# LSH attention with a spatial-gating MLP: hash rows by way of DRAM, two softmax factors on another engine, new figures in the plan

## Chip, cores, metric

One core of a Trainium2 chip runs the whole kernel. The metric is the device time in microseconds of that core, the median of several executions of the unchanged program. Engines are named as in the profile: PE (matrix products), DVE (VectorE), ACT (ScalarE), POOL (GpSimd) and SP, whose queue issues every DMA of this kernel.

## What is computed

The reference, cut to what matters (float32 attention; batch 4, 8 heads, 768 positions, head width 64; then an MLP of model width 512 and inner width 1024):

```python
q_bits = (np.einsum('bhsd,dk->bhsk', q, proj) > 0)          # 6 hash bits; k likewise
mask = q_bucket[:, :, :, None] == k_bucket[:, :, None, :]
scores = np.where(mask, scale * np.matmul(q, k.transpose(0, 1, 3, 2)), -1000000000.0)
attn = np.exp(scores - np.max(scores, axis=-1, keepdims=True))
attn = attn / (np.sum(attn, axis=-1, keepdims=True) + 1e-09)
x = np.matmul(attn, v)                                       # heads side by side
h = np.maximum(x @ w_in, 0.0); u, v = h[..., :512], h[..., 512:]
v_n = (v - mu) / np.sqrt(var + 1e-06)
out = (u * (np.einsum('ts,bsd->btd', w_spatial, v_n) + b_spatial)) @ w_out
```

## The kernel before, in words

Heads are worked on in pairs (`pair(p)`, 16 of them, four to a batch), one head on partitions 0 to 63 and one on 64 to 127. Each operand is held as a float16 high part and a low part, and a product is three products of parts that add up in PSUM. A pair first loads its q and k (`qk`, line 282), takes the hash projection on PE (`hash_`, tile `hp`), makes signs of it on DVE (line 290, tile `sg0`), scales them on ACT (line 292, tile `sg1`), and lays them out as twelve rows a head in a buffer `hr`; `rows` (line 295) does that in eight DMAs, four pieces for each of two heads. In the scores the row parts of q times those of k enter as a fourth product, which lowers every score whose buckets differ.

A pair then has six **steps** (`scores`, line 330), one for each 128 queries; 96 in all. A step is 16 score matmuls on PE (tiles `sp`); for each of two heads `cut` on DVE, which copies the scores to SBUF (`ex`) and takes their maximum (`mx`); `nb`, the maximum times a factor (line 362, on POOL, 128x2 numbers); `exp` on ACT with sums in `sm` (line 367); `ri`, the sum made ready for the reciprocal (line 369, POOL, 128x2) and the reciprocal itself (line 370, DVE); the high part of the weights on ACT (line 373, `pp`) and the low part on DVE (line 375); and `turn`, a DMA transpose per head (line 381, `pt<-pp`). After three steps `weighted` (line 384) multiplies the transposed weights with v on PE (tile `pv`) and writes `xt`. When a batch's four pairs are done, `mlp` (line 411) has 28 units of PE work for it (`vps`, `ups`, `sps`, `ops`), which the order spreads between the next batch's steps; those of the last batch stand alone at the end. The MLP's weights are loaded and split during the first batches (`weights`, line 224, tiles `raw`).

Every operation is recorded with an engine, a duration, a due key and, for a DMA, a landing time. `plan` (line 122) then plays the queues through with these figures and the sizes of the buffer rings (`RING`, line 84), always taking the ready operation with the lowest key, and what comes out is the fixed program order of all five queues. On the chip every queue runs in that order, whatever the real durations are: an instruction that waits holds up all that stand behind it on its queue. In the plan `rows` counts as one operation of 0.6 us on SP, a transpose as 1.4 us on SP with 2.0 us to land, `nb` and `ri` as 0.25 and 0.2 us on POOL. `pp` has a ring of four, so two steps' weights can wait for their transposes; `ex` has six (three steps).

Of the kernel before, what the change touches and what calls it, by code (L numbers as in the profile page):

```python
# [14 lines left out]
P = 128  # L15
D = 64
# [16 lines left out]
def lsh_attention_spatial_gating(  # L33
# [35 lines left out]

    NHR = 3  # L70
    NR = 2 * NB
    hr = [const.tile([P, 2, S], F16, name=f"hr{i}") for i in range(NHR)]
    for i, t in enumerate(hr):
# [9 lines left out]

    RING = {"sc": 2, "pv": 2, "m": 2, "hr": NHR, "qk": 1, "v32": 1, "hl": 2, "vp": 2, "sg0": 1, "sg1": 2,
            "ex": 6, "pp": 4, "pt": 4, "xt": 6, "st2": 4, "st6": 4, "v32m": 4, "vy": 2, "vn": 1, "u": 1,
            "g": 1, "sy": 2, "sm3": 2, "bs": 2, "mv": 2}
# [35 lines left out]
    def plan():  # L122


        SEM, MODE, DMA_LAT = 0.1, 0.1, 1.6
        LATE = {"PE": 0.17, "DVE": 0.09, "ACT": 0.1, "POOL": 0.05, "SP": 0.0}
# [36 lines left out]
        while done < len(ops):  # L163
            nxt = None
            for e in free:
                while free[e] <= now:
# [57 lines left out]
    def weights():  # L224
        vi, vo, vs = (x.rearrange("(c p) f -> p c f", p=P) for x in (w_in, w_out, w_sp))
        n = 0
        for src, dst, cs, lo, hi, m, f, W, key, dk in (
                (vi, wi, NPAIR, F2, DF, 256, SX, Wv, 5.0, 1.9), (vi, wi, NPAIR, 0, F2, 256, SX, Wu, 20.5, 1.0),
                (vs, ws, NT, 0, S, HS, SW, Ws, 28.0, 0.5), (vo, wo, NF, 0, DM, 256, SX, Wo, 33.5, 0.5)):
            for c in range(cs):  # L230
                for h in range(lo, hi, m):
                    job(n, src[:, c, h:h + m], [w[:, c, h:h + m] for w in dst], m, f, W, key)
                    n += 1
                    key += dk
        op("SP", 0.5, 27.0, lambda: nc.sync.dma_start(out=bt, in_=b_sp.partition_broadcast(P)), w=[Bt], land=1.0)

    def job(n, src, dst, m, f, W, key):
# [4 lines left out]

        op("SP", 0.5, key - 1.5, fetch, w=[raw], land=1.6 if m == 256 else 1.1)
        if src.dtype == F32:
# [33 lines left out]
    def pair(p):  # L278
        b, r = divmod(p, NPAIR)
        k0 = NT * (p - 1) + 0.4 if p else -40.0  # L280
        qk, v32, hl, vp, hrb, hp, s0, s1 = (Buf(t) for t in ("qk", "v32", "hl", "vp", "hr", "m", "sg0", "sg1"))
        op("SP", 0.9, k0 - 1.9, lambda: nc.sync.dma_start(out=tile_of(qk, wk, [P, 2, S], F32, f"qk{p}"), in_=kq[b, r]), w=[qk], land=2.4)

        def hash_():
            t = tile_of(hp, ps_m, [P, 512], F32, f"hp{p}")
            matmuls([(t[32 * j:32 * j + 32, :HS], pj, qk.t[:, 1 - j // 2, (j % 2) * HS:(j % 2 + 1) * HS],
                      True, True, (0, 32 * j)) for j in range(4)])
# [6 lines left out]

        def rows():
            hrb.t = hr[p % NHR]
            for e in range(2):
                for j in range(4):
                    nc.sync.dma_start(
                        out=hrb.t[D * e:D * e + NR, 1 - j // 2, (j % 2) * HS:(j % 2 + 1) * HS],  # L300
                        in_=s1.t[32 * j + 16 * e:32 * j + 16 * e + NR, :])

        op("SP", 0.6, k0 + 0.3, rows, r=[s1], w=[hrb], land=0.8)

# [10 lines left out]
        k1 = NT * p  # L315
        op("SP", 0.5, k1 - 3.0, lambda: nc.sync.dma_start(out=tile_of(v32, wk, [P, 2 * NT, D], F32, f"v32_{p}"), in_=v[b, r]), w=[v32], land=1.3)
        op("ACT", 0.74, k1 + 0.5, lambda: nc.scalar.activation(
# [12 lines left out]
    def scores(p, i, hl, hrb, pts):  # L330
# [24 lines left out]
        for e in range(2):  # L355
# [5 lines left out]
            op("DVE", 0.88, g, cut, r=[ps[e]], w=[ex[e], mx])  # L361
        op("POOL", 0.25, g, lambda: nc.gpsimd.tensor_scalar(tile_of(nb, wk, [P, 2], F32, f"nb{p}_{i}"), mx.t, -ISQ, None, op0=ALU.mult), r=[mx], w=[nb])  # L362
        for e in range(2):
# [4 lines left out]
            op("ACT", 0.92, g, exp, r=[nb], w=[ex[e], sm])  # L368
        op("POOL", 0.2, g, lambda: nc.gpsimd.tensor_scalar(tile_of(ri, wk, [P, 2], F32, f"ri{p}_{i}"), sm.t, 1e-9, 1.0 / SP, op0=ALU.add, op1=ALU.mult), r=[sm], w=[ri])  # L369
        op("DVE", 0.1, g, lambda: nc.vector.reciprocal(ri.t, ri.t), w=[ri])  # L370
        j = i % 3
        for e in range(2):
# [5 lines left out]
            def turn(e=e):  # L378
                if j == 0:
                    tile_of(pts[e], wk, [P, 2 * NT, 3, P], F16, f"pt{p}_{i}_{e}")  # L380
                nc.sync.dma_start_transpose(out=pts[e].t[:, :, j, :], in_=pp[e].t.rearrange("p g c k -> p (g c k)"))
            op("SP", 1.4, g, turn, r=[pp[e]], w=[(pts[e], j)], land=2.0)

# [27 lines left out]
    def mlp(b):  # L411
# [111 lines left out]
        def o_unit(i, key):  # L523
# [3 lines left out]
            def product():  # L527
# [87 lines left out]
```

## Time and profile before

| | us |
|---|---|
| median of 3 runs (727.54 to 729.74) | 729.18 |
| the profiled execution, whole | 725.48 |
| its span, first to last instruction | 723.7 |
| PE / DVE / ACT / POOL busy in the span | 602.5 / 528.4 / 507.4 / 200.5 |

The whole time of the profiled execution is 1.8 us more than its span, and 3.7 us below the median. Busy times are sums over stretches with different limits; the stages are read apart below. The granted clock of PE is given as a share of its full 2.4 GHz.

### The profile page before, as it was taken

To read this page: it belongs to the slowest core of one execution; us is meant where nothing else is said; L and a number is where in the kernel's file an instruction comes from. 1 tells how busy PE (TensorE), PEld (TensorE's weight loads), DVE (VectorE), ACT (ScalarE), POOL (GpSimd) and SP (SyncE) were. 2 spreads that over 40 slices of the span, in tenths; PEclk is the share of its full clock that TensorE was granted. 3 is DMA by queue.
4 is the path that set the end of the run, shared out by engine and by line. 5 is a ranking of instruction groups with operands and counts; after the bars stand their busy time and mean duration, and the time that the engine had idled before them with its cause. 6 is when DMAs were issued, how large, how long until landed. Compare 5 with 4: busy or idle time off the path is not lost. (4 is left out here: it accounts for less than half of the span.)

```text
span 723.7 us, 12276 instructions
## 1 busy us (share of the span) xinstructions
PE 602.5 (83%) x4352; PEld 302.6 (42%) x4352; DVE 528.4 (73%) x985; ACT 507.4 (70%) x905; POOL 200.5 (28%) x322
## 2 busy tenths in 40 slices
PE   2658566658888875999899989969998999989997
PEld 0224223333444432455344545534454555445553
DVE  3869788978799889857679876985788968864100
ACT  3768577878899768856777877785768778763221
POOL 2022122233144443106014420420033502302513
PEclk9998666666999985999999999989999999999999
DMA  4677988979798779886786869779856997790011
GB/s 137 178 160 155 223 178 159 224 142 236 124 237 150 176 166 217 186 177 138 135 202 126 171 126 217 162 152 181 159 112 139 178 178 131 146 202 3 1 45 43
DMA packets 317726, 111.73 MB, mean 154 GB/s; under 512 B 304224, under 2 KB 307296, under 8 KB 317664
## 3 DMA queue, kind: packets, MB, share of 16 engines
q1 hardware_dynamic: 317664, 110.94, 74.3%
q8 instruction: 34, 0.56, 0.3%
q14 instruction: 28, 0.23, 0.1%
HBM read 27.94 MB, written 6.29 MB: 47 GB/s over the span
## 5 line engine op out<-in xcount | busy, mean ns | idle before, releaser
L214 PE MATMUL sp<-hl 64*128 64x384 f16 x1152 | 169.3, 374 | 82.6 <-DVE ex L359 79.7
L375 DVE SCALAR_TENSOR_TENSOR pp<-ex,ri,pp 128x768 f16<-128x768 f32 x192 | 199.2, 1063 | 46.9 <-ACT pp L373 46.0
L373 ACT ACTIVATE pp<-ex,ri 128x768 f16<-128x768 f32 x192 | 172.3, 927 | 56.5 <-DMA pt<-pp 21.9
L367 ACT ACTIVATE ex<-ex,nb 128x768 f32<-128x768 f32 x192 | 177.5, 925 | 42.9 <-POOL nb L362 42.8
L359 DVE TENSOR_SCALAR_CACHE_REDUCE ex<-sp 128x768 f32<-128x768 f32 x192 | 179.2, 947 | 23.6 <-PE sp L214 23.3
L214 PEld LDWEIGHTS <-hl 64*128 64x128 f16 x1152 | 66.7, 103 | 171.0 <-issue 117.8
L214 PE MATMUL pv<-pt,vp 128*64 128x384 f16 x1152 | 112.7, 350 | 10.5 <-DMA pt<-pp 10.4
L214 PE MATMUL sps<-ws,vn 128*128 128x384 f16 x576 | 98.3, 328 | 0.0
L214 PE MATMUL sp<-hr 64*128 64x384 f16 x384 | 92.3, 376 | 4.1 <-DMA hr<-sg 4.1
L214 PEld LDWEIGHTS <-vp 128*64 128x64 f16 x1152 | 70.7, 118 | 54.6 <-issue 17.3
L369 POOL TENSOR_SCALAR ri<-sm 128x2 f32<-128x2 f32 x96 | 29.3, 305 | 199.6 <-ACT ex L367 192.8
L362 POOL TENSOR_SCALAR nb<-mx 128x2 f32<-128x2 f32 x96 | 37.0, 385 | 151.6 <-DVE ex L359 129.0
L214 PEld LDWEIGHTS <-vn 128*128 128x128 f16 x576 | 54.8, 98 | 41.9 <-issue 7.6
L214 PE MATMUL ops<-wo,g 128*128 128x512 f16 x288 | 66.9, 383 | 1.8 <-POOL g L520 1.0
L214 PE MATMUL ups<-xt,wi 128*128 128x384 f16 x384 | 66.0, 326 | 2.4 <-ACT vr L432 1.3
L214 PE MATMUL vps<-wi,xt 128*128 128x512 f16 x288 | 65.3, 380 | 0.6 <-ACT vr L432 0.5
L214 PEld LDWEIGHTS <-wi 128*128 128x128 f16 x384 | 36.4, 98 | 31.1 <-issue 8.0
L508 DVE SCALAR_TENSOR_TENSOR sy<-sps,bt 128x384 f32<-128x384 f32 x32 | 17.6, 551 | 42.3 <-PE sps L214 40.6
L511 POOL TENSOR_TENSOR sy<-sy,u 128x384 f32<-128x384 f32 x32 | 36.2, 1131 | 39.4 <-DVE sy L508 39.1
L471 POOL TENSOR_TENSOR vn<-vy,vn 128x512 f16<-128x512 f32 x24 | 31.3, 1313 | 48.0 <-ACT vn L468 47.9
L214 PEld LDWEIGHTS <-g 128*128 128x128 f16 x288 | 26.7, 98 | 40.0 <-issue 5.2
L214 PEld LDWEIGHTS <-xt 128*128 128x128 f16 x288 | 26.8, 98 | 37.0 <-issue 6.5
(49 smaller groups left out, 517.2 us busy)
## 6 DMA issues: line engine op xcount, KB each, us to landing
qk<-kq SPq DMA_DIRECT2D x16, 768.0 KB
v<-v SPq DMA_DIRECT2D x16, 384.0 KB
out<-o SPq DMA_DIRECT2D x24, 256.0 KB
raw<-w_in SPq DMA_DIRECT2D x16, 256.0 KB
pt<-pp SPq DMA_TRANSPOSE x192
raw<-w_sp SPq DMA_DIRECT2D x12, 192.0 KB
hr<-sg SPq DMA_DIRECT2D x128, 9.0 KB
raw<-w_out SPq DMA_DIRECT2D x8, 256.0 KB
```

The source lines that it names most:

```text
L214: nc.tensor.matmul(out_, lhsT=lhsT, rhs=rhs, start=start, stop=stop, **({} if pos is None else {"tile_position": pos}))
L359: nc.vector.tensor_scalar(tile_of(ex[e], wk, [P, 2, HS], F32, f"ex{p}_{i}_{e}"), ps[e].t[:, :, :HS], -float(2 ** 27), None, op0=ALU.max, o ...
L362: op("POOL", 0.25, g, lambda: nc.gpsimd.tensor_scalar(tile_of(nb, wk, [P, 2], F32, f"nb{p}_{i}"), mx.t, -ISQ, None, op0=ALU.mult), r=[mx], ...
L367: nc.scalar.activation(ex[e].t, ex[e].t, AF.Exp, bias=nb.t[:, e:e + 1], scale=ISQ, accum_out=sm.t[:, e:e + 1])
L369: op("POOL", 0.2, g, lambda: nc.gpsimd.tensor_scalar(tile_of(ri, wk, [P, 2], F32, f"ri{p}_{i}"), sm.t, 1e-9, 1.0 / SP, op0=ALU.add, op1=AL ...
L373: op("ACT", 0.83, g, lambda e=e: nc.scalar.activation(tile_of(pp[e], wk, [P, 2, 2, HS], F16, f"pp{p}_{i}_{e}")[:, 0], ex[e].t, AF.Copy, sc ...
L375: op("DVE", 0.93, g, lambda e=e: nc.vector.scalar_tensor_tensor(out=pp[e].t[:, 1], in0=ex[e].t, scalar=ri.t[:, e:e + 1], in1=pp[e].t[:, 0] ...
L471: op("POOL", 1.11, key, lambda i=i, y=y: nc.gpsimd.tensor_tensor(out=vn[1].t[:, i], in0=y.t, in1=vn[0].t[:, i], op=ALU.subtract), r=[y], w ...
L508: op("DVE", 0.47, key, lambda: nc.vector.scalar_tensor_tensor(out=tile_of(y, wk, [P, HS], F32, f"sy{b}_{d}_{h}"), in0=ps.t[:, :HS], scalar ...
L511: op("POOL", 0.96, key, lambda: nc.gpsimd.tensor_mul(y.t, y.t, u[h].t[:, d]), r=[(u[h], d)], w=[y])
```

## The change

1. The signs `sg1` are written to DRAM by one DMA (`dr`, line 298) and read back by two, one for each head, each with four pieces of row in one access pattern (line 302). The two halves of `hr` become operations of their own in the plan, and q and k take each other's place among the projection's four row groups to suit that pattern. `hr` has two buffers in place of three, `sg1` one in place of two.
2. `nb` (line 366) and `ri` (line 373) go from POOL to DVE.
3. In the plan: SP issues at 0.6 us (loads), 1.5 us (transposes, before 1.4); a transpose lands in 1.7 us (before 2.0), the general DMA latency is 1.3 us (before 1.6).
4. The ring of `xt` has seven buffers in place of six.

```diff
+    dr = ctx.enter_context(tc.tile_pool(name="dr", bufs=1, space=bass.MemoryType.DRAM))
...
-    NHR = 3
+    NHR = 2
...
-    RING = {"sc": 2, "pv": 2, "m": 2, "hr": NHR, "qk": 1, "v32": 1, "hl": 2, "vp": 2, "sg0": 1, "sg1": 2,
-            "ex": 6, "pp": 4, "pt": 4, "xt": 6, "st2": 4, "st6": 4, "v32m": 4, "vy": 2, "vn": 1, "u": 1,
+    RING = {"sc": 2, "pv": 2, "m": 2, "hr": NHR, "qk": 1, "v32": 1, "hl": 2, "vp": 2, "sg0": 1, "sg1": 1, "dr": 2,
+            "ex": 6, "pp": 4, "pt": 4, "xt": 7, "st2": 4, "st6": 4, "v32m": 4, "vy": 2, "vn": 1, "u": 1,
...
-        SEM, MODE, DMA_LAT = 0.1, 0.1, 1.6
+        SEM, MODE, DMA_LAT = 0.1, 0.1, 1.3
...
-                        o.end = dma + 0.3
+                        o.end = dma + 0.25
...
-        op("SP", 0.9, k0 - 1.9, lambda: nc.sync.dma_start(out=tile_of(qk, wk, [P, 2, S], F32, f"qk{p}"), in_=kq[b, r]), w=[qk], land=2.4)
+        op("SP", 0.6, k0 - 1.9, lambda: nc.sync.dma_start(out=tile_of(qk, wk, [P, 2, S], F32, f"qk{p}"), in_=kq[b, r]), w=[qk], land=2.4)
-            matmuls([(t[32 * j:32 * j + 32, :HS], pj, qk.t[:, 1 - j // 2, (j % 2) * HS:(j % 2 + 1) * HS],
+            matmuls([(t[32 * j:32 * j + 32, :HS], pj, qk.t[:, j // 2, (j % 2) * HS:(j % 2 + 1) * HS],
...
-        def rows():
+        d = Buf("dr")
+        op("SP", 0.6, k0 + 0.3, lambda: nc.sync.dma_start(out=tile_of(d, dr, [P, HS], F16, f"dr{p}"), in_=s1.t), r=[s1], w=[d], land=0.5)
+        def rows(e):
             hrb.t = hr[p % NHR]
-            for e in range(2):
-                for j in range(4):
-                    nc.sync.dma_start(
-                        out=hrb.t[D * e:D * e + NR, 1 - j // 2, (j % 2) * HS:(j % 2 + 1) * HS],
-                        in_=s1.t[32 * j + 16 * e:32 * j + 16 * e + NR, :])
-        op("SP", 0.6, k0 + 0.3, rows, r=[s1], w=[hrb], land=0.8)
+            nc.sync.dma_start(
+                out=hrb.t[D * e:D * e + NR].rearrange("r g (c k) -> r (g c) k", c=2),
+                in_=d.t.rearrange("(j r) k -> r j k", j=4)[16 * e:16 * e + NR])
+        for e in range(2):
+            op("SP", 0.6, k0 + 0.3, lambda e=e: rows(e), r=[d], w=[(hrb, e)], land=0.3)
...
-        op("POOL", 0.25, g, lambda: nc.gpsimd.tensor_scalar(tile_of(nb, wk, [P, 2], F32, f"nb{p}_{i}"), mx.t, -ISQ, None, op0=ALU.mult), r=[mx], w=[nb])
+        op("DVE", 0.08, g, lambda: nc.vector.tensor_scalar(tile_of(nb, wk, [P, 2], F32, f"nb{p}_{i}"), mx.t, -ISQ, None, op0=ALU.mult), r=[mx], w=[nb])
                 nc.scalar.activation(ex[e].t, ex[e].t, AF.Exp, bias=nb.t[:, e:e + 1], scale=ISQ, accum_out=sm.t[:, e:e + 1])
-        op("POOL", 0.2, g, lambda: nc.gpsimd.tensor_scalar(tile_of(ri, wk, [P, 2], F32, f"ri{p}_{i}"), sm.t, 1e-9, 1.0 / SP, op0=ALU.add, op1=ALU.mult), r=[sm], w=[ri])
+        op("DVE", 0.08, g, lambda: nc.vector.tensor_scalar(tile_of(ri, wk, [P, 2], F32, f"ri{p}_{i}"), sm.t, 1e-9, 1.0 / SP, op0=ALU.add, op1=ALU.mult), r=[sm], w=[ri])
...
-            op("SP", 1.4, g, turn, r=[pp[e]], w=[(pts[e], j)], land=2.0)
+            op("SP", 1.5, g, turn, r=[pp[e]], w=[(pts[e], j)], land=1.7)
```

Loads of weights and v and stores of the output also count 0.6 us on SP in place of 0.5. The plan places everything anew. Three places of the program order follow; a name like `pp_4_0` is tile, step of the pair and head, and the number behind it is the tile's own.

SP's queue late in the pair before `hr_74` is written, before (`hr_74` holds the rows of pair 4, `sg_4` its signs):

```order
L241 DMA raw_889<-w_in 128x256
L381 DMA_TRANSPOSE pt_3_0_796<-pp_4_0_861 128x12x128
L381 DMA_TRANSPOSE pt_3_1_803<-pp_4_1_886 128x12x128
L381 DMA_TRANSPOSE pt_3_0_796<-pp_5_0_905 128x12x128
L381 DMA_TRANSPOSE pt_3_1_803<-pp_5_1_910 128x12x128
L299 DMA hr_74<-sg_4_958 12x384 x8
L241 DMA raw_998<-w_in 128x256
L381 DMA_TRANSPOSE pt_0_0_1007<-pp_0_0_991 128x12x128
L241 DMA raw_1012<-w_in 128x256
L381 DMA_TRANSPOSE pt_0_1_1021<-pp_0_1_1002 128x12x128
L381 DMA_TRANSPOSE pt_0_0_1007<-pp_1_0_1044 128x12x128
```

and now, from the first half of pair 3's rows to pair 4's signs:

```order
L302 DMA hr_76<-dr_636 12x4x384
L385 DMA_TRANSPOSE pt_3_0_814<-pp_3_0_796 128x12x128
L385 DMA_TRANSPOSE pt_3_1_822<-pp_3_1_802 128x12x128
L302 DMA hr_76<-dr_636 12x4x384
L283 DMA qk_879<-kq 128x1536
L242 DMA raw_908<-w_in 128x256
L242 DMA raw_915<-w_in 128x256
L385 DMA_TRANSPOSE pt_3_0_814<-pp_4_0_906 128x12x128
L385 DMA_TRANSPOSE pt_3_1_822<-pp_4_1_912 128x12x128
L385 DMA_TRANSPOSE pt_3_0_814<-pp_5_0_939 128x12x128
L385 DMA_TRANSPOSE pt_3_1_822<-pp_5_1_942 128x12x128
L298 DMA dr_986<-sg_4_984 128x384
```

Eight issues in one piece have become two reads between the transposes and loads, and the one write of the signs stands by itself (that of pair 3, `dr_636`, ten queue rows ahead of this piece).

SP's queue at the program's start, before:

```order
L235 DMA bt<-b_sp 128x768
L299 DMA hr_73<-sg_0_107 12x384 x8
L282 DMA qk_120<-kq 128x1536
L316 DMA v_1_123<-v 128x768
L241 DMA raw_133<-w_in 128x256
L241 DMA raw_158<-w_in 128x256
L282 DMA qk_207<-kq 128x1536
L299 DMA hr_74<-sg_1_201 12x384 x8
```

and now:

```order
L298 DMA dr_109<-sg_0_107 128x384
L283 DMA qk_114<-kq 128x1536
L320 DMA v_1_117<-v 128x768
L242 DMA raw_127<-w_in 128x256
L302 DMA hr_75<-dr_109 12x4x384
L242 DMA raw_135<-w_in 128x256
L298 DMA dr_153<-sg_1_151 128x384
L302 DMA hr_75<-dr_109 12x4x384
L283 DMA qk_159<-kq 128x1536
```

The second half of pair 0's rows now stands behind the signs of pair 1, and pair 1's q and k are no longer behind eight row issues.

DVE's queue around the last step of pair 10, before (`ex_5` with `mx_5` is the cut of that step, `ri_4` the reciprocal of the step ahead of it):

```order
L359 TENSOR_SCALAR ex_5_0_4622,mx_5_4621<-sp_5_0_4571 128x768
L313 SCALAR_TENSOR_TENSOR hl_4619<-qk_4108,hl_4619 128x2x768
L370 RECIPROCAL ri_4_4666<-ri_4_4666 128x2
L359 TENSOR_SCALAR ex_5_1_4670,mx_5_4621<-sp_5_1_4572 128x768
L508 SCALAR_TENSOR_TENSOR sy_2_0_4676<-sps_2_0_4597,bt 128x384
L375 SCALAR_TENSOR_TENSOR pp_4_0_4674<-ex_4_0_4554,ri_4_4666,pp_4_0_4674 128x768
L375 SCALAR_TENSOR_TENSOR pp_4_1_4678<-ex_4_1_4558,ri_4_4666,pp_4_1_4678 128x768
L405 SCALAR_TENSOR_TENSOR xt_4706<-pv_0_4629,xt_4706 128x384
L359 TENSOR_SCALAR ex_0_0_4730,mx_0_4729<-sp_0_0_4686 128x768
L370 RECIPROCAL ri_5_4734<-ri_5_4734 128x2
```

and now, from that step's cuts on:

```order
L363 TENSOR_SCALAR ex_5_0_4651,mx_5_4650<-sp_5_0_4604 128x768
L363 TENSOR_SCALAR ex_5_1_4654,mx_5_4650<-sp_5_1_4605 128x768
L317 SCALAR_TENSOR_TENSOR hl_4647<-qk_4084,hl_4647 128x2x768
L366 TENSOR_SCALAR nb_5_4676<-mx_5_4650 128x2
L512 SCALAR_TENSOR_TENSOR sy_3_0_4678<-sps_3_0_4627,bt 128x384
L363 TENSOR_SCALAR ex_0_0_4685,mx_0_4684<-sp_0_0_4658 128x768
L363 TENSOR_SCALAR ex_0_1_4690,mx_0_4684<-sp_0_1_4659 128x768
L373 TENSOR_SCALAR ri_5_4693<-sm_5_4682 128x2
L366 TENSOR_SCALAR nb_0_4695<-mx_0_4684 128x2
L374 RECIPROCAL ri_5_4693<-ri_5_4693 128x2
```

`nb_5`, which ACT's exponentials of that step wait for, stood on POOL's queue and now stands behind a subtraction for `hl`; `ri_5` and its reciprocal have `nb_0` between them.

## Rows read from the trace of the kernel before

**Rows 1.** Windows by stage: PE, PEld, DVE, ACT, POOL busy us; clock, DMA share, GB/s.
```profile
25.00:300.00 275.00, 197.68 (x1419) 94.57 (x1420) 231.55 (x451) 217.17 (x398) 82.74 (x133) 0.81 0.90 183
300.00:650.00 350.00, 329.24 (x2505) 169.14 (x2500) 272.03 (x485) 260.87 (x454) 91.01 (x157) 0.98 0.79 159
650.00:723.70 73.70, 66.52 (x384) 36.13 (x384) 13.63 (x31) 17.99 (x37) 22.09 (x22) 1.00 0.08 27
```

**Rows 2.** Windows of the score matmuls alone (PE x: sixteen a step).
```profile
25.00:300.00 275.00, 101.62 (x683) 80.60 (x172) 0.81 0.90 183
300.00:650.00 350.00, 82.01 (x825) 97.29 (x208) 0.98 0.79 159
```

**Rows 3.** Waits, 25:300: engine line, waited for, us in total, times, longest.
```profile
PE sp L214 <- DVE ex L359: 67.8, 48, 5.4
...
ACT ex L367 <- POOL nb L362: 15.9, 17, 2.3
ACT pp L373 <- DMA pt<-pp: 15.0, 11, 3.2
...
DVE ri L370 <- POOL ri L369: 3.4, 5, 1.9
```

**Rows 4.** Waits, 300:650.
```profile
DVE ri L370 <- POOL ri L369: 26.9, 22, 2.7
ACT ex L367 <- POOL nb L362: 26.8, 16, 2.9
...
PE pv L214 <- DMA pt<-pp: 4.9, 3, 3.2
```

**Rows 5.** Timeline, 60:82: start, us, engine, operation, tiles [idle before, releaser].
```profile
64.98 6.25 SPq L299 DMA_DIRECT2D hr<-sg  x8
...
75.26 0.94 ACT L373 ACTIVATE pp<-ex,ri 128x768 f16<-128x768 f32 x1 [2.48 <-DMA pt<-pp]
...
76.23 1.02 DVE L375 SCALAR_TENSOR_TENSOR pp<-ex,ri,pp 128x768 f16<-128x768 f32 x1 [2.46 <-ACT pp L373]
...
78.18 0.48 PE L214 MATMUL sp<-hl 64*128 64x384 f16 x1 [5.24 <-DVE ex L359]
```

**Rows 6.** Timeline of PE, 462:500.
```profile
468.53 3.12 PE L214 MATMUL pv<-pt,vp 128*64 128x384 f16 x36
...
485.37 0.53 PE L214 MATMUL pv<-pt,vp 128*64 128x384 f16 x1 [3.22 <-DMA pt<-pp]
487.07 4.46 PE L214 MATMUL pv<-pt,vp 128*64 128x384 f16 x35 [1.18 <-DMA pt<-pp]
```

**Rows 7.** Timeline of SP, 455:500.
```profile
469.94 6.45 SPq L299 DMA_DIRECT2D hr<-sg  x8
```

**Rows 8.** The hr tile's row issues: ns min/median/max, first and last start.
```profile
L299 SPq DMA_DIRECT2D hr<-sg x128: 713/714/994, 9.4 to 553.6; - x128
```

**Rows 9.** Groups: busy us, mean ns of one, idle before and releasers.
```profile
L359 DVE TENSOR_SCALAR_CACHE_REDUCE ex<-sp 128x768 f32<-128x768 f32 x192 | 179.2, 947 | 23.6 <-PE sp L214 23.3
...
L362 POOL TENSOR_SCALAR nb<-mx 128x2 f32<-128x2 f32 x96 | 37.0, 385 | 151.6 <-DVE ex L359 129.0 <-DVE ri L370 14.6 <-DVE ve L453 4.5
...
L369 POOL TENSOR_SCALAR ri<-sm 128x2 f32<-128x2 f32 x96 | 29.3, 305 | 199.6 <-ACT ex L367 192.8 <-DVE ex L359 4.8 <-PE pv L214 0.4
L313 DVE SCALAR_TENSOR_TENSOR hl<-qk,hl 128x1536 f16<-128x1536 f32 x16 | 28.0, 1751 | 0.9 <-ACT hl L310 0.8
...
L359 DVE DVE_READ_ACCUMULATOR ex<-sp 128x1 f32 x192 | 15.6, 81 | 0.0
L370 DVE RECIPROCAL ri<-ri 128x2 f32<-128x2 f32 x96 | 15.4, 160 | 31.3 <-POOL ri L369 30.3
```

**Rows 10.** Timeline of SP, 0:75.
```profile
9.42 6.23 SPq L299 DMA_DIRECT2D hr<-sg  x8
...
31.21 4.19 SPq L381 DMA_TRANSPOSE pt<-pp  x2
35.51 6.09 SPq L299 DMA_DIRECT2D hr<-sg  x8
```

More of the change, by code (lines that the diff above doesn't have):

```diff
@@ L234, in weights @@
                     key += dk
-        op("SP", 0.5, 27.0, lambda: nc.sync.dma_start(out=bt, in_=b_sp.partition_broadcast(P)), w=[Bt], land=1.0)
+        op("SP", 0.6, 27.0, lambda: nc.sync.dma_start(out=bt, in_=b_sp.partition_broadcast(P)), w=[Bt], land=1.0)
     def job(n, src, dst, m, f, W, key):
@@ L241, in fetch @@
             nc.sync.dma_start(out=tile_of(raw, wk, [P, m], src.dtype, f"raw{n}"), in_=src)
-        op("SP", 0.5, key - 1.5, fetch, w=[raw], land=1.6 if m == 256 else 1.1)
+        op("SP", 0.6, key - 1.5, fetch, w=[raw], land=1.6 if m == 256 else 1.1)
         if src.dtype == F32:
@@ L315, in pair @@
         k1 = NT * p
-        op("SP", 0.5, k1 - 3.0, lambda: nc.sync.dma_start(out=tile_of(v32, wk, [P, 2 * NT, D], F32, f"v32_{p}"), in_=v[b, r]), w=[v32], land=1.3)
+        op("SP", 0.6, k1 - 3.0, lambda: nc.sync.dma_start(out=tile_of(v32, wk, [P, 2 * NT, D], F32, f"v32_{p}"), in_=v[b, r]), w=[v32], land=1.3)
         op("ACT", 0.74, k1 + 0.5, lambda: nc.scalar.activation(
@@ L535, in o_unit @@
                 tile_of(o, wk, [P, DM], F32, f"o{b}_{i}"), ps.t, AF.Copy, scale=1.0 / (SX * SX)), r=[ps], w=[o])
-            op("SP", 0.5, key, lambda: nc.sync.dma_start(out=out[b, i * P:(i + 1) * P, :], in_=o.t), r=[o], land=1.5)
+            op("SP", 0.6, key, lambda: nc.sync.dma_start(out=out[b, i * P:(i + 1) * P, :], in_=o.t), r=[o], land=1.5)
         n = 0
```

## The prediction, made before the changed kernel was run

> **What bounds the kernel now.** I read the stages first, since the page's shares are averages over unlike ones. In the windows by stage [rows 1] three things can be seen. From 650 us on PE is busy 66.5 of 73.7 us: the last batch's MLP, which nothing here touches. From 300 to 650 us PE is busy 329.2 of 350, so PE sets the pace and only its 20.8 idle us can be had. From 25 to 300 us nobody is full: PE 197.7, DVE 231.6, ACT 217.2 of 275, with the DMA engines at a share of 0.90 and PE at a granted clock of 0.81. The score matmuls [rows 2], at sixteen a step, say how far each stage gets: 683/16 = 43 steps early, 825/16 = 52 late.
>
> Next I read who waits in the early stage [rows 3]. PE waits 67.8 us for DVE's cuts, so PE is not its limit. ACT waits 15.0 us for transposes to free `pp`. What makes these late stands in the timeline [rows 5]: SP issues the rows of a pair in one block of 6.25 us from 64.98 on; transposes stand behind it; ACT then idles 2.48 us for `pt<-pp`, DVE 2.46 behind ACT, PE 5.24 behind DVE's cut. In the late stage the same block [rows 7], 6.45 us from 469.94 on, reaches PE itself [rows 6]: `pv` waits 3.22 and 1.18 us for its transposes, and 35 of its matmuls then take 4.46 us where the 36 at 468.53 took 3.12.
>
> **The change part by part.** The sum is made against the profiled execution, 725.5 us; the median of the runs is 729.2, so the difference is carried over to that.
>
> *Row issues (A).* Removed: 8 issues a pair, at 0.714 us median [rows 8]. Added: 3, at the same price as the nearest row, 2.1 us with the same spread of unit cost; so SP gets back some 4.0 of the block's 6.2 us, and what is left no longer comes in one piece. Early, seven blocks lie between 25 and 300 us besides the one at 24.46, as read off SP's timeline, whose first ones are in [rows 10]. Lower bound of the gain: 0, if the transfers and not their issue are late. Upper: 7 x 4.0 = 28 us, if SP paces the stage. Between them lies what ACT waits, 15.0 us, of which 4.0/6.2 would go: 9.7. The sample shows DVE and PE losing as much as ACT or more for one block, so I take 14, half way up, nearer to ACT's row. Late, PE's waits of 4.9 us for transposes [rows 4] and the 1.3 us by which `pv` ran longer make 6.2; 4.0/6.2 of that is 4.0. Bounds 0 and 6.2.
>
> The way through DRAM puts two transfers where one was, and the reads wait for the write. The rows are wanted at the next pair's first step, six steps of more than 6 us (275/43) after the signs, so this lies beside other work; if that cover were gone, the first score product would wait, as at the start. There the program order has pair 0's second read behind pair 1's signs. That costs up to one load of q and k, which I bound by a block's length, 6.2 us; against it, the block at 35.51 that kept step 1's transposes back after the first ones at 31.21 is gone [rows 10], 6.1 us. Taken: 0, bounds -6 and +6. The read also waits for the pair two back, `hr` having two buffers; behind it on SP stand transposes. Since scores run ahead of their transposes by two of the three steps that `ex` holds, I take 0.
>
> *Small factors (B).* Moved: 2 x 96 instructions of POOL (385 and 305 ns in the mean) become DVE instructions. The trace has none of them on DVE; the nearest rows are the accumulator's read of 81 ns and the reciprocal of the same shape, 160 ns [rows 9]. Middle: 120 ns, 0.24 us a step. Early: 43 x 0.24 = +10.3 us on the engine that is fullest there, bounds 7 and 14. Late: 52 x 0.24 = 12.5 us into 78 us of DVE idle time [rows 1], taken at 0; if that cover fails, up to +12. With POOL's turn the waits for it end: early ACT 15.9 and DVE 3.4 us [rows 3], late 26.8 and 26.9 [rows 4]. But in the new order something else stands in the way: of 96 `nb`, 24 have at least 0.9 us of other DVE work between them and their second cut, and of 96 reciprocals 49 have as much between them and their `ri` (counted in the order, with a cut at 0.95 and an `hl` subtraction at 1.75 us [rows 9]). So I set the early waits against each other, 0, and late, where PE seldom waits on this chain, take -2.
>
> *The plan's figures and the seventh `xt`.* These change only the order. In the new PE order batch 0's MLP starts after step 24 in place of 26 and its last unit ends after step 51 in place of 50; from step 52 on the MLP's units stand within two steps of where they stood, and the tail is the same. 0, bounds inside those of the late stage.
>
> **Sum:** early -14 + 10 = -4; late -4 - 2 = -6; start 0. 725.5 - 10 = 715.5 for a profiled execution, 729.2 - 10 = **719** for the median. With B's ends and A between 10 and 23 the likeliest case reaches from 710 to 726.
>
> **Rivals.**
> 1. *SP paced the early stage.* Each block gives back its whole 4.0 us: -28 + 10 - 6 = -24, 705. For it: in both samples the stalls begin with SP's block [rows 5, 7]. Against: DVE must then be busy 242 of 251 us, 96%.
> 2. *The transfers, not their issue, are late.* Then A is 0 in both stages: +10 - 2 = +8, 737, slower. For it: the DMA share of 0.90 early. Against: it fell to 0.79 late and a block still cost PE 4.4 us [rows 6]. A rule of the Trainium skill speaks for this one and against the change: the page "DMA: Bandwidth & Descriptors", section "Issuing engines are not separate DMA queues", says that the sequencer's time to start a DMA is usually small beside the DMA itself. By that rule this rival would be the likeliest; the trace disagrees, with 6.25 us for eight issues of 12 rows each.
> 3. *DVE's line takes POOL's place, slower.* A late `ri` or `nb` holds up ACT's next pass, and an `ri` ahead of a `nb` ties two steps together. Early, 24 reciprocals and 13 `nb` stand behind at least a cut of 0.95 us: 35 us, against the 19 us of waits for POOL that end. If all shows, +16: -14 + 10 + 16 - 6 = +6, 735. It decides once what ACT and DVE lose there passes 19 us by more than the 10 that A leaves over. For it: PE's 67.8 us behind DVE's cuts, and the full DVE. Against: ACT has other work in most of these places.
> 4. *Nothing to be seen.* A and B cancel everywhere: within 0.3% of 729.2, which is 2.2 us and about what a measurement of this kernel can tell from no change.
> That the change does not do what it says is excluded by the order: three issues a pair and no `nb` or `ri` on POOL.
>
> **Chances.** Forecast 0.50, rival 1 0.14, rival 2 0.10, rival 3 0.13, rival 4 0.11, and 0.02 for something slower still. Faster: 0.50 + 0.14 = 0.64. Same: 0.11. Slower: 0.25. The range from 704 to 738 takes in the rivals' times; rival 1 beyond 704 and rivals 2 and 3 beyond 738 are left out, together under 2 in 10.
>
> **What would show each step right or wrong.** A: SP's timeline without blocks of 6 us, three row DMAs of some 0.7 us a pair, ACT's early wait for `pt<-pp` down from 15.0 to about 5 us, PE reaching step 45 some 4 us earlier. B: DVE busy up by 15 to 31 us, its new instructions at 80 to 160 ns; POOL busy down by 66; no ACT wait for POOL's `nb`, and one for DVE's `nb` below the 43 us (15.9 + 26.8) that POOL's cost. Wrong: PE's wait for `pv`'s transposes unchanged (rival 2), or ACT's waits for `nb` and `ri` above what they were for POOL (rival 3), or a start whose first transposes come after 37 us.

## The result and the profile after

The changed kernel takes 709.41 us (median of 4 runs, 703.75 to 710.90), the kernel before 729.42 us beside it (4 runs, 727.54 to 729.74): a ratio of 0.9717, 95% interval 0.9658 to 0.9776. That is 20 us faster where 10 were forecast. The time lies in the range (704 to 738), but just under the likeliest case's own (710 to 726). The profiled execution took 710.9 us with a span of 709.1, so it is one of the slower ones; against the profiled execution before, its span is 14.6 us shorter.

Windows by stage of the kernel after, in the columns of [rows 1]:

```profile
25.00:300.00 275.00, 212.06 (x1549) 104.49 (x1546) 244.64 (x544) 227.54 (x418) 44.95 (x46) 0.80 0.92 188
300.00:650.00 350.00, 325.77 (x2459) 172.40 (x2457) 281.98 (x589) 253.93 (x441) 61.05 (x55) 0.98 0.79 155
```

and of its score matmuls alone, as in [rows 2]:

```profile
25.00:300.00 275.00, 97.18 (x716) 84.86 (x179) 0.80 0.92 188
300.00:650.00 350.00, 77.81 (x800) 94.87 (x202) 0.98 0.79 155
```

Early, PE is now busy 212.1 us instead of 197.7, at the same granted clock, and gets through 716 score matmuls instead of 683: two steps more. Counted along PE's timeline, sixteen score matmuls a step and the first step called 0, step 45 starts at 297.2 us where it started at 311.0 (13.8 earlier), and the last score matmul at 617.8 where it was 636.7 (18.9 earlier). So most of the gain was made early.

The groups of the kernel after (columns as in [rows 9]):

```profile
L371 ACT ACTIVATE ex<-ex,nb 128x768 f32<-128x768 f32 x192 | 177.4, 924 | 34.5 <-DVE nb L366 34.2
L377 ACT ACTIVATE pp<-ex,ri 128x768 f16<-128x768 f32 x192 | 170.1, 925 | 38.7 <-issue 22.4 <-DVE ri L374 8.3 <-ACT ex L371 2.8
L215 PE MATMUL pv<-pt,vp 128*64 128x384 f16 x1152 | 121.2, 363 | 16.8 <-DMA pt<-pp 15.6 <-DMA dr<-sg 1.1
...
L373 DVE TENSOR_SCALAR ri<-sm 128x2 f32<-128x2 f32 x96 | 22.9, 238 | 6.2 <-ACT ex L371 6.1
...
L366 DVE TENSOR_SCALAR nb<-mx 128x2 f32<-128x2 f32 x96 | 17.2, 179 | 0.4
L215 PE MATMUL hp<-qk,hc 128*32 128x384 f32 x128 | 16.9, 606 | 17.9 <-DMA qk<-kq 17.7 <-ACT vr L436 0.2
L374 DVE RECIPROCAL ri<-ri 128x2 f32<-128x2 f32 x96 | 15.4, 160 | 0.4
```

Its busy times over the whole span, and what is left of ACT's wait for transposes between 25 and 300 us (columns as in [rows 3]):

```profile
PE 600.4 (85%) x4352; PEld 308.1 (43%) x4352; DVE 549.4 (77%) x1177; ACT 506.7 (71%) x905; POOL 128.9 (18%) x129
ACT pp L377 <- DMA pt<-pp: 0.2, 1, 0.2
```

ACT's wait for transposes to free `pp`, 15.0 us early [rows 3], no longer stands in its row: 0.2 us are left. The two small factors count 22.9 and 17.2 us on DVE, at 238 and 179 ns in the mean (164 and 168 in the median), more than the 80 to 160 ns that were assumed. But they overlap other records of DVE, which add up to 625.5 us where DVE is busy 549.4, and its busy time rises by 21.0 us only, from 528.4. DVE no longer waits for POOL before the reciprocal (26.9 us late alone, [rows 4]), and ACT waits 34.2 us for DVE's `nb`, less than the 15.9 + 26.8 it waited for POOL's. PE waits longer for transposes before `pv`, 15.6 us.

SP's timeline after, 55 to 95 us, over the stretch that answers to [rows 5], and below it the two tiles of the rows (ns min/median/max):

```profile
64.98 0.87 SPq L298 DMA_DIRECT2D dr<-sg  x1
66.49 7.91 SPq L385 DMA_TRANSPOSE pt<-pp  x4
...
82.26 0.36 SPq L302 DMA_DIRECT2D hr<-dr  x1
82.71 3.45 SPq L385 DMA_TRANSPOSE pt<-pp  x2
86.26 0.80 SPq L302 DMA_DIRECT2D hr<-dr  x1
87.16 0.37 SPq L283 DMA_DIRECT2D qk<-kq  x1
```

```profile
L302 SPq DMA_DIRECT2D hr<-dr x32: 311/400/925, 12.6 to 551.0; - x32
L298 SPq DMA_DIRECT2D dr<-sg x16: 326/844/910, 8.7 to 524.5; - x16
```

The block of 6.25 us is gone. By the medians a pair's rows take SP 0.844 + 2 x 0.400 = 1.64 us instead of 8 x 0.714 = 5.71: 4.07 us less a pair, 65 us over 16 pairs.

### The profile page after: what moved, and what is told of

The parts are those of the page before. It is cut to its first block, busy times and chain, and to the rows that moved or that the text cites. A ratio compares the mean times of both kernels' runs of the same rounds, so it can differ in the third digit from the quotient of the medians.

```text
span 709.1 us, 12175 instructions
## 1 busy us (share of the span) xinstructions
PE 600.4 (85%) x4352; PEld 308.1 (43%) x4352; DVE 549.4 (77%) x1177; ACT 506.7 (71%) x905; POOL 128.9 (18%) x129
## 5 line engine op out<-in xcount | busy, mean ns | idle before, releaser
L379 DVE SCALAR_TENSOR_TENSOR pp<-ex,ri,pp 128x768 f16<-128x768 f32 x192 | 197.6, 1064 | 31.5 <-ACT pp L377 31.2
L215 PE MATMUL sp<-hl 64*128 64x384 f16 x1152 | 159.6, 361 | 65.3 <-DVE ex L363 65.2
L371 ACT ACTIVATE ex<-ex,nb 128x768 f32<-128x768 f32 x192 | 177.4, 924 | 34.5 <-DVE nb L366 34.2
L363 DVE TENSOR_SCALAR_CACHE_REDUCE ex<-sp 128x768 f32<-128x768 f32 x192 | 180.3, 949 | 23.2 <-PE sp L215 22.4
L377 ACT ACTIVATE pp<-ex,ri 128x768 f16<-128x768 f32 x192 | 170.1, 925 | 38.7 <-issue 22.4
L215 PE MATMUL pv<-pt,vp 128*64 128x384 f16 x1152 | 121.2, 363 | 16.8 <-DMA pt<-pp 15.6
L215 PEld LDWEIGHTS <-hl 64*128 64x128 f16 x1152 | 64.1, 101 | 144.8 <-issue 112.9
L215 PEld LDWEIGHTS <-vp 128*64 128x64 f16 x1152 | 78.4, 122 | 61.5 <-issue 28.6
L215 PE MATMUL sp<-hr 64*128 64x384 f16 x384 | 87.2, 365 | 2.2 <-DMA hr<-dr 2.0
L512 DVE SCALAR_TENSOR_TENSOR sy<-sps,bt 128x384 f32<-128x384 f32 x32 | 17.7, 554 | 39.6 <-PE sps L215 39.5
L215 PEld LDWEIGHTS <-xt 128*128 128x128 f16 x288 | 26.8, 98 | 37.1 <-issue 7.2
L524 POOL TENSOR_TENSOR g<-sy,g 128x384 f16<-128x384 f32 x32 | 31.1, 972 | 34.9 <-ACT g L521 34.9
L215 PEld LDWEIGHTS <-hr 64*128 64x128 f16 x384 | 29.3, 104 | 18.1 <-DMA hr<-dr 2.4
```

The source lines that it names most:

```text
L215: nc.tensor.matmul(out_, lhsT=lhsT, rhs=rhs, start=start, stop=stop, **({} if pos is None else {"tile_position": pos}))
L363: nc.vector.tensor_scalar(tile_of(ex[e], wk, [P, 2, HS], F32, f"ex{p}_{i}_{e}"), ps[e].t[:, :, :HS], -float(2 ** 27), None, op0=ALU.max, o ...
L371: nc.scalar.activation(ex[e].t, ex[e].t, AF.Exp, bias=nb.t[:, e:e + 1], scale=ISQ, accum_out=sm.t[:, e:e + 1])
L377: op("ACT", 0.83, g, lambda e=e: nc.scalar.activation(tile_of(pp[e], wk, [P, 2, 2, HS], F16, f"pp{p}_{i}_{e}")[:, 0], ex[e].t, AF.Copy, sc ...
L379: op("DVE", 0.93, g, lambda e=e: nc.vector.scalar_tensor_tensor(out=pp[e].t[:, 1], in0=ex[e].t, scalar=ri.t[:, e:e + 1], in1=pp[e].t[:, 0] ...
L512: op("DVE", 0.47, key, lambda: nc.vector.scalar_tensor_tensor(out=tile_of(y, wk, [P, HS], F32, f"sy{b}_{d}_{h}"), in0=ps.t[:, :HS], scalar ...
```

## Experiments

Two theories were set against each other first: that SP's time in the blocks of row issues was the loss, and that the transfers were, or that the gain came from another part of the change. In a kernel whose order a planner makes, an edit of the plan changes the order of all queues as well. So three kernels below keep the order of every queue (two_of_eight that of the kernel before; five_more and same_order that of the changed one); these price what they change. In the others the order moves too, and what an order alone can do to the time shows further down: 14 us less in one case, 9 more in another.

### Two of the eight row issues

The kernel before, in its own order, with one piece of row for each head; the other six are left out, so that the hash lowers only part of the scores:

```diff
-                for j in range(4):
+                for j in (0,):
```

> The kernel before in its own program order on all five queues, with two of a pair's eight row issues (one for each head); the other three quarters of the rows are not laid out, so the hash masks only part of the scores. SP gets back 6 x 0.73 = 4.4 us a pair and nothing else changes. Theory S (the block of issues on SP held the transposes up): faster by 10 to 20 us, about 713, with ACT's wait for transposes well below 21.9 us. Rival F (the gain comes from the new order and the plan's figures): within 3 us of before. Rival D (it comes from moving the small factors): within 3 us of before.

700.36 us (699.38 to 702.07) against 728.13: ratio 0.9604 (0.9567 to 0.9640), 27.8 us faster, more than the 10 to 20 expected. Groups of this kernel:

```profile
L373 ACT ACTIVATE pp<-ex,ri 128x768 f16<-128x768 f32 x192 | 171.5, 925 | 34.0 <-DVE ri L370 11.3 <-issue 10.2 <-ACT ex L367 7.7
L214 PE MATMUL pv<-pt,vp 128*64 128x384 f16 x1152 | 110.3, 345 | 3.3 <-DMA pt<-pp 3.2
```

With the block cut to a quarter, ACT's wait for `pt<-pp` goes and PE's before `pv` falls from 10.4 us to 3.2. Taken away are 6 x 0.714 x 16 = 68.5 us of SP's time: 0.41 us of the kernel's time for each us. As three quarters of the row transfers are gone as well, this run alone doesn't part issue from transfer.

### Five more issues

The changed kernel in its own order, with five small loads a pair ahead of the second row read, into tiles that nobody reads:

```diff
+            if e:
+                for t in spare:
+                    nc.sync.dma_start(out=t, in_=hconst[0:NR, :])
...
```

> The changed kernel in its own program order, with five more small DMAs a pair (12 rows of 136 bytes from DRAM into spare tiles) issued ahead of the second read of the rows; the plan does not know of them. They give SP back some 5 x 0.73 = 3.6 us of issue time a pair and next to no transfer. Theory S: slower than the changed kernel by 8 to 16 us, 717 to 725. Rival F or D: within 3 us of the changed kernel. Rival T (transfers, not their issue, were late): within 3 us as well.

723.64 us (721.29 to 727.87, 10 runs), ratio 0.9942 (0.9912 to 0.9972). The tile of these loads, and the projection's group:

```profile
L305 SPq DMA_DIRECT2D spare<-hconst x80: 297/362/1520, 17.9 to 562.8; - x80
```

```profile
L216 PE MATMUL hp<-qk,hc 128*32 128x384 f32 x128 | 17.1, 612 | 25.6 <-DMA qk<-kq 25.4 <-ACT vr L440 0.2
```

By the median, 0.362 us in place of the 0.73 expected, 80 issues are 29 us on SP, and 33 by their sum; the time rises by 14.2 us, 0.4 to 0.5 for each us. The loads are 12 rows of 136 bytes, and nothing waits for them; what stands behind them on SP waits: for q and k PE's wait grows from 17.7 us (the same group of the kernel after, above) to 25.4. Issue time with next to no transfer, and none that anyone needs, so takes back most of the gain; what so small a transfer itself holds up was not told apart from its issue.

### The rows alone

The kernel before with the way through DRAM, two `hr` and one `sg1` buffers, and nothing else of the change.

```diff
...
-        def rows():
...
+        d = Buf("dr")
+        op("SP", 0.6, k0 + 0.3, lambda: nc.sync.dma_start(out=tile_of(d, dr, [P, HS], F16, f"dr{p}"), in_=s1.t), r=[s1], w=[d], land=0.5)
...
+        def rows(e):
...
```

> The kernel before with the rows by way of DRAM alone: three issues, two buffers of hr, one of sg1; small factors on POOL, old figures of the plan, six xt. Theory S: 10 to 18 us faster than before, about 715, and less than 6 us slower than the changed kernel. Rival D: most of the gain missing, above 722. Rival F: likewise above 722.

708.47 us (707.43 to 712.94), ratio 0.9714 (0.9673 to 0.9754): as much as the whole change gains, with the factors still on POOL and the old figures, but in an order of its own. In its profiled execution (712.9 us) step 45 starts only 3.1 us earlier than before, at 307.9, and the last score matmul 13.8 earlier, at 622.9: where along the kernel the gain shows is a matter of the order.

### The factors back on POOL

The changed kernel with `nb` and `ri` planned and run on POOL.

```diff
-        op("DVE", 0.08, g, lambda: nc.vector.tensor_scalar(tile_of(nb, wk, [P, 2], F32, f"nb{p}_{i}"), mx.t, -ISQ, None, op0=ALU.mult), r=[mx], w=[nb])
+        op("POOL", 0.25, g, lambda: nc.gpsimd.tensor_scalar(tile_of(nb, wk, [P, 2], F32, f"nb{p}_{i}"), mx.t, -ISQ, None, op0=ALU.mult), r=[mx], w=[nb])
...
```

> The changed kernel with nb and ri back on POOL (0.25 and 0.2 us in the plan, as before), all else as changed. Theory S: 0 to 8 us faster than the changed kernel, 702 to 709, since DVE loses 40 us of small instructions where it is the fullest engine. Rival D: slower by 8 us or more, 718 and above, with ACT waiting some 40 us for POOL's nb again.

705.09 us (702.85 to 707.42), ratio 0.9666 (0.9621 to 0.9711): some 4 us below the changed kernel, with intervals that overlap, and in another order.

### The factors on DVE alone

The kernel before with `nb` and `ri` planned and run on DVE (the same lines, the other way).

> The kernel before with nb and ri on DVE alone; rows in eight issues, old figures, six xt. Theory S, with the move a cost (no_dve ran 4 us faster than the changed kernel): 0 to 8 us slower than before, 728 to 737. Rival D: faster than before by 3 us or more.

749.99 us (745.47 to 754.32), ratio 1.0258 (1.0183 to 1.0334): 20 us slower, where at most 8 were expected. Its groups:

```profile
L367 ACT ACTIVATE ex<-ex,nb 128x768 f32<-128x768 f32 x192 | 177.5, 925 | 54.3 <-DVE nb L362 53.7
...
L214 PE MATMUL pv<-pt,vp 128*64 128x384 f16 x1152 | 131.6, 384 | 38.2 <-DMA pt<-pp 32.6 <-ACT ex L367 5.7
```

ACT waits 53.7 us for `nb` (in the kernel before 42.8 for POOL's) and PE 32.6 for transposes before `pv` (10.4). Rival 3's mechanism shows in these waits; but the order moved as well, and how much of the 20 us is the order's is not told apart here. In the changed kernel's order the move cost nothing (same_order, below).

### Without the figures, without the seventh `xt`

Two kernels: the changed one with all the old issue and landing figures, and the changed one with a ring of six.

```diff
-        SEM, MODE, DMA_LAT = 0.1, 0.1, 1.3
+        SEM, MODE, DMA_LAT = 0.1, 0.1, 1.6
...
-            "ex": 6, "pp": 4, "pt": 4, "xt": 7, "st2": 4, "st6": 4, "v32m": 4, "vy": 2, "vn": 1, "u": 1,
+            "ex": 6, "pp": 4, "pt": 4, "xt": 6, "st2": 4, "st6": 4, "v32m": 4, "vy": 2, "vn": 1, "u": 1,
```

> The changed kernel with the old figures in the plan (issues 0.5, 0.9 and 1.4 us, transposes landing in 2.0, latency 1.6). Theory S: within 4 us of the changed kernel, 705 to 713, with PE's waits for pv's transposes smaller, since a longer landing in the plan puts pv later. Rival F: slower by 5 us or more.

> The changed kernel with six xt in place of seven. Both theories that do not rest on it: within 3 us of the changed kernel. If the seventh xt carries a part of the gain: slower by 4 us or more, since batch 0's MLP starts two steps later again.

706.97 us (701.67 to 707.26), ratio 0.9672 (0.9611 to 0.9734), and 707.42 (706.64 to 708.26), ratio 0.9696 (0.9643 to 0.9748). Neither differs measurably from the changed kernel's 0.9717: no gain of these two parts shows, as far as single orders can tell. The seventh `xt` was not tried on the kernel before.

### A later landing of q and k in the plan

The changed kernel, factors on POOL, with q and k taken to land 4.0 us after their issue (the lines that put the factors on POOL are those of "The factors back on POOL").

```diff
-        op("SP", 0.6, k0 - 1.9, lambda: nc.sync.dma_start(out=tile_of(qk, wk, [P, 2, S], F32, f"qk{p}"), in_=kq[b, r]), w=[qk], land=2.4)
+        op("SP", 0.6, k0 - 1.9, lambda: nc.sync.dma_start(out=tile_of(qk, wk, [P, 2, S], F32, f"qk{p}"), in_=kq[b, r]), w=[qk], land=4.0)
```

> The changed kernel with nb and ri on POOL, and with q and k landing in the plan in 4.0 us in place of 2.4 (in the trace of the changed kernel 4.4 us pass from the issue of pair 1's q and k at 9.80 to their first use at 14.20). The hash products then stand later on PE's queue: pair 1's behind pair 0's first scores. If PE's 17.7 us of waits for q and k are on the path: 3 to 10 us faster than no_dve, 695 to 702. If they are hidden: within 3 us of no_dve, 702 to 708.

690.68 us (689.58 to 691.10), ratio 0.9464 (0.9413 to 0.9515): faster than both kernels, and by more than expected. But the order did not become what was expected: pair 1's projection still stands ahead of pair 0's first scores, which start at 15.63 us (15.66 in the changed kernel); only pair 2's moved, behind the second step. The next two kernels ask whether the figure did that: the same figure in the changed kernel, and in the kernel before.

> The changed kernel with one figure changed, q and k taken to land 4.0 us after their issue in the plan instead of 2.4; the small factors stay on VectorE. If what was left of the start and of the order is the projection standing ahead of its loads on PE's queue (17.7 us of PE waits for qk in the changed kernel), the gain seen with the factors on POOL comes back here less some 4 us for the factors: 691 to 700 us, ratio to the kernel before 0.947 to 0.96, PE's wait for qk below 12 us. If that gain was a lucky order that the figure happened to find, this kernel stays near the changed one, 703 to 711 us, ratio 0.965 to 0.975.

> The kernel before, blocks and all, with only that figure changed to 4.0 us. The kernel before waits 10.3 us on PE for qk, so if this wait is what the figure takes away the most to be had is some 10 us: ratio 0.986 to 1.0. If the figure's 14 us have another source, a better order of all queues, as much as 0.98 comes out; if the blocks of row issues eat what the order wins, 1.0 or above.

711.12 us (710.37 to 711.61), ratio 0.9775 (0.9746 to 0.9805), and 736.18 us (735.18 to 737.74), ratio 1.0123 (1.0095 to 1.0151). The figure brings nothing to the one and costs the other 9 us. So the 690.7 us belong to that one order, which this figure happened to lead to with the factors on POOL; what in the order does it stays open. For the rest of this study it gives a measure: a figure in the plan can move the time, through the order, by 14 us down or 9 up.

### The plan told of the block

The kernel before, eight issues kept, with their real time in the plan:

```diff
-        op("SP", 0.6, k0 + 0.3, rows, r=[s1], w=[hrb], land=0.8)
+        op("SP", 6.2, k0 + 0.3, rows, r=[s1], w=[hrb], land=0.8)
```

> The kernel before with the eight row issues kept and only the plan told what they take on SP, 6.2 us instead of 0.6. The theory that SP's time itself is short in a block: the plan can put transposes ahead of the block, but the 6.2 us must still be spent while transposes come due, so at most a part of the 28 us that the two-of-eight kernel won comes back: 720 to 730 us, ratio 0.987 to 1.0. The rival that only the plan's ignorance was at fault, its order having left no room: 700 to 712 us, ratio 0.96 to 0.976, as good as the whole change.

732.19 us (731.15 to 734.30), ratio 1.0072 (1.0047 to 1.0097). Planning for the block didn't help here. This speaks against the rival by which only the plan's ignorance was at fault; as it is one order among many, it doesn't rule it out.

### The factors on POOL in the changed kernel's order

`nb` and `ri` run on POOL but are planned as if on DVE, so that PE, ACT and SP keep the changed kernel's order row for row:

```diff
-        op("DVE", 0.08, g, lambda: nc.vector.tensor_scalar(tile_of(nb, wk, [P, 2], F32, f"nb{p}_{i}"), mx.t, -ISQ, None, op0=ALU.mult), r=[mx], w=[nb])
+        op("DVE", 0.08, g, lambda: nc.gpsimd.tensor_scalar(tile_of(nb, wk, [P, 2], F32, f"nb{p}_{i}"), mx.t, -ISQ, None, op0=ALU.mult), r=[mx], w=[nb])
...
```

> The changed kernel with the 2 x 96 small factors issued on POOL, but planned as if on VectorE: PE, ACT and SP keep the changed kernel's order row for row, and VectorE keeps it with these 192 rows taken out. The plan's order scatters the time by some 10 us, so only this prices the move itself. As the prediction put it (+10 early, -2 late), VectorE's 40.1 us of new instructions cost 8 us: then this kernel runs in 701 us, ratio to the kernel before 0.961, VectorE busy 21 us less. Rival: the factors lie in VectorE's waits and cost nothing, 0.97 to 0.973. Second rival: the two extra hand-overs a step to POOL cost more than VectorE's time saves, since in this order nothing was placed to cover them: 0.976 or above, with ACT waiting longer for POOL's nb than the 34.2 us it waited for VectorE's.

708.23 us (706.09 to 710.97), ratio 0.9726 (0.9695 to 0.9757): the same as the changed kernel, and not the 0.961 by which the prediction's price would have shown. Its busy times, then its groups:

```profile
PE 597.9 (84%) x4352; PEld 306.0 (43%) x4352; DVE 526.3 (74%) x985; ACT 506.7 (72%) x905; POOL 187.6 (26%) x321
...
L379 DVE SCALAR_TENSOR_TENSOR pp<-ex,ri,pp 128x768 f16<-128x768 f32 x192 | 197.5, 1064 | 37.7 <-ACT pp L377 37.1
L363 DVE TENSOR_SCALAR_CACHE_REDUCE ex<-sp 128x768 f32<-128x768 f32 x192 | 179.7, 950 | 26.7 <-PE sp L215 26.3
L371 ACT ACTIVATE ex<-ex,nb 128x768 f32<-128x768 f32 x192 | 177.5, 925 | 36.7 <-POOL nb L366 36.5
...
L374 DVE RECIPROCAL ri<-ri 128x2 f32<-128x2 f32 x96 | 15.4, 161 | 17.6 <-POOL ri L373 17.1
```

DVE is busy 526.3 us instead of 549.4, 23 us less, and idles about as much more: 17.1 us ahead of the reciprocal for POOL (6.1 us for ACT ahead of `ri` in the changed kernel), 37.1 behind ACT's `pp` (31.2), 26.3 behind PE (22.4). What DVE saves in work it loses in waits, about half of them hand-overs to POOL. The second expectation, that the factors cost nothing, holds.

## Why the prediction was right, and where not

**The reason was right: SP's blocks were the loss.** The markers of the row issues came out but for sizes: no block of 6 us, three issues a pair, ACT's early wait for `pt<-pp` down from 15.0 to 0.2 us (about 5 were named), step 45 earlier by 13.8 us (some 4 were named, since B's early cost was counted in). The saving of some 4.0 us a block was right too (4.07 by the medians). Three runs carry it: fewer issues in an unchanged order give 27.8 us, more issues in an unchanged order take 14 away, and the rows alone, in an order of their own, give the whole 20. The changed kernel moves more bytes than before, 113.3 MB where it was 111.7, since each row goes twice, and is faster: rival 2, by which transfers and not issue were late, falls. The Trainium skill's rule behind that rival (page "DMA: Bandwidth & Descriptors", section "Issuing engines are not separate DMA queues") says that the sequencer's time is usually small beside the DMA itself. On this one queue it was not small enough to leave out: some 30 us of added issue time that no transfer hung on cost 14 us.

**A, the row issues, was sized well early and too low late.** Against the kernel before, two_of_eight starts step 45 at 292.3 us instead of 311.0 and its last score matmul at 610.7 instead of 636.7: 18.7 us early, another 7.3 late. In the kernel before, step 3 and the last score matmuls start here:

```profile
31.23 0.50 PE L214 MATMUL sp<-hl 64*128 64x384 f16 x1
...
636.74 0.33 PE L214 MATMUL sp<-hr 64*128 64x384 f16 x2
```

The early 18.7 hold more than the seven blocks from 25 us on that the prediction counted. At step 3, which starts ahead of the first of the seven, two_of_eight is 5.0 us ahead (26.2 and 31.2), so that much goes with the blocks at 9.42 and 24.46, which the prediction left to the start, and 13.7 with the seven. It takes away 4.3 us a pair and the change 4.07, so A should be worth 13 early and 7 late, by scaling. The prediction took 14 and 4, out of 0 to 28 and 0 to 6.2. Its way to the 14, ACT's waiting row enlarged because DVE and PE lost more than ACT, was sound; late, PE's waits for transposes did not hold all that the blocks cost. Rival 1's 28 early did not come.

**The start was put at 0 and took time.** PE's timeline after, 5 to 53 us:

```profile
14.22 1.51 PE L215 MATMUL hp<-qk,hc 128*32 128x384 f32 x8 [6.84 <-DMA qk<-kq]
15.66 1.14 PE L215 MATMUL sp<-hl 64*128 64x384 f16 x6
...
19.45 0.50 PE L215 MATMUL sp<-hr 64*128 64x384 f16 x1 [2.05 <-DMA hr<-dr]
...
22.66 1.51 PE L215 MATMUL hp<-qk,hc 128*32 128x384 f32 x8 [1.43 <-DMA qk<-kq]
...
32.93 0.48 PE L215 MATMUL sp<-hl 64*128 64x384 f16 x1 [2.32 <-DVE ex L363]
```

and two_of_eight's, the same stretch and its last score matmuls:

```profile
9.79 1.14 PE L214 MATMUL sp<-hl 64*128 64x384 f16 x6 [2.40 <-DVE hl L313]
...
15.09 1.50 PE L214 MATMUL hp<-qk,hc 128*32 128x384 f32 x8 [1.67 <-DMA qk<-kq]
...
26.22 0.50 PE L214 MATMUL sp<-hl 64*128 64x384 f16 x1
...
610.71 0.33 PE L214 MATMUL sp<-hr 64*128 64x384 f16 x2
```

In the changed order the second pair's projection stands ahead of the first scores on PE and waits 6.84 us for its q and k, whose load SP issues only at 9.80, behind the first row write. The first scores start at 15.66 instead of 9.79, and then wait 2.05 us for row reads. The prediction had seen the second read behind the next pair's signs, but not this wait on PE; and it counted the block at 35.51 twice, among the seven and as what makes up for the loss here. At step 3 the changed kernel is 1.7 us behind the kernel before (32.9 and 31.2) and 6.7 behind two_of_eight (26.2); at the last score matmul it is 7.1 behind that one (617.8 and 610.7). Against the 26 us that two_of_eight gains this is the largest thing the change gives back; that the 7.1 are the same loss, carried through, is likely but not shown. The marker set for the start, first transposes after 37 us, did not catch it: they came at 31.10, as before (31.21), but two_of_eight has them at 23.47. An order with that projection behind the first scores was not run; in qk_late, meant as one, it still stands ahead of them.

**B, the factors on DVE, is the step that failed: +10 early and -2 late were put, and 0 was measured** (same_order), to within some 5 us. The work was sized well: DVE's busy time rises by 21.0 us against the kernel before and 23.1 against same_order, where 23 were assumed; the 40.1 us that the instructions' own records add up to overlap others. B's other markers came out too (POOL down by 71.6 us where 66 were named, ACT's wait for `nb` 34.2, below 43), yet the time did not move. They told of the move, not of its price. The step counted the instructions as time added to the fullest engine, and set the ended waits for POOL against new ones at 0 early. But DVE is not full: it idles 24 to 48 us behind ACT's `pp` in all these kernels, and same_order shows its hand-overs to POOL and the other waits worth as much idle time as the new work fills. By stages, in the two profiled executions, the factors on DVE make step 45 3.1 us later (297.2 and 294.1), and at the last score matmul both are level (617.8 and 617.6): the signs were right, and the early size was not. So rival 3 did not come true, in this order; dve_only shows that another order can bring its waits.

**The sum.** In steps' starts: the start +1.7, A by scaling -13 and -7, B 0, together -18; measured -18.9 at the last score matmul. The forecast, -14 + 10 - 6 = -10, came out too small mainly because B's +8 was not there; the late A was 3 short, and the start took 1.7 of that back. There is luck in it too: two things that the prediction did not count, the 5.0 us of the first two blocks and the 6.7 lost at the start, nearly cancel; without that loss 709 us would be some 703, just below the range. And the likeliest case is not what its own ends give: A 10 to 23 and B 7 to 14 reach from 707 to 727, not from 710 to 726, and by that the measured time lies in it.

**One marker was badly chosen.** PE's unchanged wait for `pv`'s transposes was named as a sign for rival 2. It rose, from 10.4 to 15.6 us, and the time fell. That PE, no longer late itself, now arrives at `pv` before its transposes is likely but not shown: in rows_only the same wait fell to 4.1 us, with the same gain.

**The tail, put at no change, grew by 4.3 us in the profiled execution** (91.3 us from the last score matmul to the end, before 87.0). PE's timeline at the end, after:

```profile
617.66 0.47 PE L215 MATMUL sp<-hr 64*128 64x384 f16 x2
618.05 0.35 PE L215 MATMUL pv<-pt,vp 128*64 128x384 f16 x1
619.61 3.08 PE L215 MATMUL pv<-pt,vp 128*64 128x384 f16 x35 [1.20 <-DMA pt<-pp]
622.62 7.94 PE L215 MATMUL vps<-wi,xt 128*128 128x512 f16 x36
633.13 0.32 PE L215 MATMUL pv<-pt,vp 128*64 128x384 f16 x1 [2.56 <-DMA pt<-pp]
634.93 5.84 PE L215 MATMUL pv<-pt,vp 128*64 128x384 f16 x35 [1.48 <-DMA pt<-pp]
```

and the same of the kernel before:

```profile
650.59 0.32 PE L214 MATMUL pv<-pt,vp 128*64 128x384 f16 x1 [1.19 <-DMA pt<-pp]
652.26 3.09 PE L214 MATMUL pv<-pt,vp 128*64 128x384 f16 x35 [1.35 <-DMA pt<-pp]
```

The order is the same, but the last transposes come 1.4 us later behind PE, and the 35 matmuls that then follow take 5.84 us instead of 3.09. The windows after give the granted clock there (columns of [rows 1]):

```profile
630.00:635.00 5.00, 0.96 (x6) 0.28 (x6) 3.42 (x11) 1.98 (x5) 0.28 (x1) 0.87 0.89 171
635.00:641.00 6.00, 6.00 (x37) 3.64 (x38) 1.36 (x1) 0.35 (x2) 1.99 (x2) 0.54 0.00 0
```

0.54 of full speed, near the lower level of 1.2 GHz, after PE had been busy 0.96 of the 5 us from 630 on. In the kernel before it stayed at 1.00 over the same matmuls:

```profile
652.50:655.30 2.80, 2.80 (x36) 2.16 (x33) 0.77 (x2) 1.14 (x2) 1.75 (x2) 1.00 0.00 0
```

That is 2.7 of the 4.3 us.

## What to carry to other kernels

Add up what a queue spends on issuing, block by block, and look at what stands behind a block: many small DMAs issued in one piece delay every later transfer of that queue, and cutting 65 us of issue time in blocks of 6 was worth more here than all else in the change. Price a moved small operation by the hand-overs that end as well as by its own time; on an engine with idle time around it, it can be free. Where a planner makes the order, try a part in an unchanged order, as a changed figure alone moved this kernel by 14 us down and 9 up.

## What the runs showed of the hardware

The price of issuing a DMA on SP depends on what it is and on what stands ahead. The eight pieces of rows from SBUF to SBUF took at least 0.713 us each [rows 8]. Rows to and from DRAM took either 0.3 to 0.5 or 0.8 to 0.9 us, and the dear ones are those issued right behind a transpose: in SP's timeline above 0.87 and 0.80 behind transposes, 0.36 (rows) and 0.37 (q and k) not. In the whole trace of the changed kernel, of 60 plain DMAs issued within 1 us behind a transpose 46 took over 0.7 us (median 0.84), of 74 issued behind another plain DMA 3 did. What makes them dear is not shown.

An instruction on 128x2 numbers (`nb` and `ri`) takes DVE 179 and 238 ns in the mean in the changed kernel and POOL 347 and 253 in the same order; in the median 168 and 164 against 214 and 192. The gap between the engines is smaller than the plan's 0.08 against 0.25 and 0.2 us.
